# A fused attention and Fourier kernel: PV with v as the stationary operand, diagonal score blocks sharing columns, transfers in pairs, and a newly searched order

## The chip, the cores and the metric

One core of one Trainium2 chip. The metric is the device time of one execution in microseconds (us). With one core, runs are compared by the granted clock of the tensor engine (TensorE) that the profile gives beside each: a run of the kernel before at clock 1.00 takes about 246.8 us, those at 0.993 took 248.2 to 252.0 us. What a lower clock goes with in the profiles is shown below; the slower runs of the kernel before were not profiled themselves. Runs over 1.5% above the fastest of their kernel are called slow, and ratios use the fast ones alone. Engines are named as the profile does: PE is TensorE's matmuls, PEld its weight loads, DVE VectorE, ACT ScalarE, POOL GpSimd.

## The reference, cut to what matters

```python
x = A_x                                             # 2048 tokens x 640, bf16
g = sigmoid((x * gate_w).sum(-1, keepdims=True))    # a gate for each token
a = attention(x)       # 32 heads of 20; four segments of 512 tokens, causal inside a segment
b = irfft2(rfft2(x) * (w_r + 1j * w_i))             # over tokens and channels
return g * a + (1 - g) * b

# attention, for each segment s:
logits = qs @ ks.T * scale + mask;  p = softmax(logits);  a_dot = p @ vs
a_mem = (phi(qs) @ M) / (phi(qs) @ z + 1e-6)        # M, z: sums over the earlier segments
o = sigmoid(beta) * a_mem + (1 - sigmoid(beta)) * a_dot
M, z = M + phi(ks).T @ vs, z + phi(ks).sum()        # at the end: out = o @ wo
```

## The kernel before

The kernel is straight-line code for five engines. It carries its own list scheduler: each operation is described once, with its inputs, outputs and a typed-in duration, and a long list named ORDER, found by a search, says in which order each engine gets its operations. The scheduler works out from the durations when each one should start, and places buffers accordingly. It knows a delay between engines, a price for changing the tiling of TensorE, and some VectorE operations that it does not place beside GpSimd's.

```python
HOP = 70.0
COST = {(0, 1): 94.0, (0, 2): 94.0, (1, 0): 110.0, ...}     # changes of tiling, ns
def schedule(self, pools, order, nsem=56):
    ...                                 # t: when inputs, bank and engine are free
    occ, lat = o.alts[e][1:]            # the typed-in duration
    if e == "pe" and o.emode != mode:
        occ += self.COST[mode, o.emode]
    free[e] = o.t1 = t + occ
```

Durations are typed in like this (matmuls, then one operation of another engine):

```python
cost = sum(c * PECOL + 0.75 if mode > 0 else max(c * PECOL + 2.8, 25.4) for _, c in items)
...
fix0, per0, late = {"act": (65, 0.833, 110.0), "dve": (67, 1.04, 68.0), "pool": (100, 0.945, 50.0)}[eng]
```

Attention works on pairs of groups of four heads. A score unit fills four PSUM banks, the exponential reads all four, GpSimd masks the triangles, and PV multiplies with the exponentials as stationary operand, 40 matmuls of 21 columns a group:

```python
POOLS = {"qk": [0, 1, 2, 3], "gen": [4, 5, 6, 7]}
for pr in range(4):
    for u, parts in enumerate(self.UNITS):
        self.qk_unit(s, pr, u, parts)          # scores, Exp, masks
    for g in (2 * pr, 2 * pr + 1):
        self.pv_group(s, g)
# the Exp, the mask of one diagonal block, and one PV product:
e.activation(dst(), src(), ACT.Exp, scale=SC)
e.affine_select(ex[.. 4 heads, 128 columns ..], same, [[0, 4], [1, P]], ALU.is_ge, 0.0, ...)
th = (psum[.. 21 columns ..], ex[.. 128 x 128 ..], va[.. 21 columns of head 4*g+hh ..])
```

(The last three lines are shortened; the whole kernel follows.)

The softmax here doesn't subtract the row's maximum and nothing guards it: scores larger than these inputs give would overflow.

## Time and profile before

The median of the first three runs was 246.92 us (246.74 to 249.36).

| | before |
|---|---|
| span of the profiled run, granted clock | 244.2 us, 1.000 |
| exponentials | 80, 150.3 us |
| masks | 128, 81.0 us |
| tensor instructions (matmuls and weight loads) | 7404 |
| PE waits for "issue" in the whole span | 0.2 us in each of two groups of lines |

### The profile page before, as it was taken

To read this page: it belongs to the slowest core of one execution; us is meant where nothing else is said; L and a number is where in the kernel's file an instruction comes from. 1 tells how busy PE (TensorE), PEld (TensorE's weight loads), DVE (VectorE), ACT (ScalarE), POOL (GpSimd) and SP (SyncE) were. 2 spreads that over 40 slices of the span, in tenths; PEclk is the share of its full clock that TensorE was granted. 3 is DMA by queue.
4 is the path that set the end of the run, shared out by engine and by line. 5 is a ranking of instruction groups with operands and counts; after the bars stand their busy time and mean duration, and the time that the engine had idled before them with its cause. 6 is when DMAs were issued, how large, how long until landed. Compare 5 with 4: busy or idle time off the path is not lost.

```text
span 244.2 us, 8905 instructions
## 1 busy us (share of the span) xinstructions
PE 233.1 (95%) x3702; PEld 139.8 (57%) x3702; DVE 198.8 (81%) x534; ACT 201.6 (83%) x204; POOL 132.2 (54%) x200
## 2 busy tenths in 40 slices
PE   7999999999999999999978999999899999999994
PEld 2344575557556457645644475645555667667683
DVE  1489997988999898979999999989999975643643
ACT  2088889999998998999987998888899878798820
POOL 8421861362648484455876385646567656407610
PEclk9999999999999999999999999999999999999999
DMA  7998866696493656756442546313442969586224
GB/s 185 328 358 231 218 172 169 205 182 172 138 192 92 168 128 150 226 164 200 109 104 71 144 137 182 94 59 111 118 100 71 203 144 97 79 123 116 77 62 131
DMA packets 55880, 36.71 MB, mean 150 GB/s; under 512 B 31792, under 2 KB 52128, under 8 KB 55840
## 3 DMA queue, kind: packets, MB, share of 16 engines
q1 hardware_dynamic: 54144, 35.32, 58.4%
q10 hardware_dynamic: 1696, 0.82, 1.2%
q8 instruction: 29, 0.48, 0.8%
q14 instruction: 11, 0.09, 0.1%
HBM read 19.86 MB, written 9.71 MB: 121 GB/s over the span
## 4 chain that ended last, share of the span: by engine, by line
PE 72%; DVE 16%; DMA 5%; ACT 4%; issue 2%; SPq 0%; DVEq 0%
PE psum L498 64%; PE psum L496 8%; DVE Pt L1287 4%; ACT ex L1137 3%; DMA xT<-in_A_x_dram 2%; DMA oT<-o_scr 2%; DVE Cp L509 2%; DVE Yt L1292 1%; DVE qu L509 1%; ACT et L1010 1%; DVE va L1045 1%; DVE Bt L509 1%; DVE on L1172 1%; DVE on L1177 0%; DVE phk L1021 0%
## 5 line engine op out<-in xcount | busy, mean ns | idle before, releaser
L1137 ACT ACTIVATE ex<-psum 128x2048 bf16<-128x2048 f32 x80 | 150.3, 1878 | 15.8 <-PE psum L498 14.8
L1140 POOL TENSOR_SCALAR_AFFINE_SELECT ex<-ex 128x512 bf16<-128x512 bf16 x128 | 81.0, 653 | 70.5 <-ACT ex L1137 66.7
L498 PEld LDWEIGHTS psum<-va,ex 128*128 128x128 bf16 x1280 | 39.0, 96 | 5.8 <-issue 1.3
L498 PE MATMUL psum<-va,ex 128*128 128x21 bf16 x1280 | 41.1, 172 | 0.1
L498 PE MATMUL psum<-xT,wk 128*128 128x512 bf16 (+1 forms) x140 | 33.3, 380 | 0.6 <-DMA xT<-in_A_x_dram 0.6
L498 PE MATMUL psum<-xT,wq 128*128 128x512 bf16 (+1 forms) x135 | 32.2, 380 | 1.2 <-DVE Bt L509 1.2
L498 PE MATMUL psum<-qp,kp 20*128 20x384 bf16 (+3 forms) x512 | 31.7, 301 | 0.7 <-ACT ex L1137 0.2
L498 PE MATMUL psum<-wv,xT 128*128 128x500 bf16 (+1 forms) x160 | 31.9, 300 | 0.2
L1287 DVE TENSOR_TENSOR Pt<-psum,Wt 128x642 bf16<-128x642 f32 x32 | 25.4, 822 | 0.8 <-PE psum L498 0.5
L496 PE MATMUL psum<-wo,oT 128*32 128x320 bf16 x480 | 23.0, 300 | 0.2 <-issue 0.2
L498 PEld LDWEIGHTS psum<-qp,kp 20*128 20x128 bf16 x512 | 9.0, 92 | 18.3 <-ACT ex L1137 9.6
L509 DVE CAST ot<-psum 128x320 bf16<-128x320 f32 x21 | 9.9, 489 | 11.6 <-PE psum L496 8.4
L498 PEld LDWEIGHTS psum<-wv,xT 128*128 128x128 bf16 x160 | 13.3, 97 | 10.0 <-DVE Ac L509 0.8
L498 PE MATMUL psum<-big,Ac 128*128 128x321 bf16 (+2 forms) x96 | 17.9, 256 | 0.8 <-DVE Cp L509 0.4
L1045 DVE TENSOR_TENSOR va<-psum,ebx 128x500 bf16<-128x500 f32 (+1 forms) x32 | 15.2, 484 | 3.5 <-PE psum L498 2.8
L498 PE MATMUL psum<-tt,Yt 128*128 128x256 bf16 (+1 forms) x96 | 17.0, 274 | 0.4 <-DVE qu L509 0.2
L1292 POOL TENSOR_TENSOR Yt<-Pt 128x321 bf16<-128x321 bf16 x18 | 13.4, 757 | 7.2 <-DVE Pt L1287 4.6
L509 DVE CAST qu<-psum 128x512 bf16<-128x512 f32 x20 | 13.6, 686 | 3.4 <-PE psum L498 3.2
L1333 DVE TENSOR_TENSOR G<-eo,psum 128x320 bf16<-128x320 f32 x32 | 14.9, 479 | 1.7 <-PE psum L496 0.9
L498 PEld LDWEIGHTS psum<-xT,wk 128*128 128x128 bf16 (+1 forms) x140 | 9.9, 97 | 10.9 <-issue 2.3
L1177 POOL TENSOR_TENSOR on<-on,mem 128x320 bf16<-128x320 bf16 x16 | 12.8, 806 | 5.8 <-DVE on L1172 5.8
L1172 DVE TENSOR_TENSOR on<-psum,rs 128x320 bf16<-128x320 f32 x32 | 15.3, 481 | 0.6
(85 smaller groups left out, 379.9 us busy)
## 6 DMA issues: line engine op xcount, KB each, us to landing
tt<-tab_tt SPq DMA_DIRECT2D x16, 256.0 KB, 3.3
xsb<-in_A_x_dram SPq DMA_DIRECT2D x8, 320.0 KB
kp<-k_scr SPq DMA_DIRECT2D x28, 80.0 KB
qp<-q_scr SPq DMA_DIRECT2D x28, 80.0 KB
o_scr<-on SPq DMA_DIRECT2D x12, 160.0 KB
out_dram<-ot SPq DMA_DIRECT2D x12, 160.0 KB
q_scr<-qu SPq DMA_DIRECT2D x6, 256.0 KB
k_scr<-qu SPq DMA_DIRECT2D x6, 256.0 KB, 3.9
```

The costliest lines, as they stand in the source:

```text
L496: h = e.matmul(dst, wt, r_, start=st, stop=sp_, **{**kw, "tile_position": (0, q), "skip_group_check": True})
L498: h = e.matmul(o_, l_, r_, start=st, stop=sp_, **kw)
L509: alts["dve"] = (lambda e: e.tensor_copy(dst(), src()), 67 + 1.04 * n, 68.0)
L1010: self.one("act", lambda e: e.activation(et.ap(0, [1, L]), qsl(), ACT.Exp), L, [qb], [b("et", pi_)], late, name="phi_exp")
L1045: self.one("dve", lambda e: e.tensor_tensor(va.ap(i * H * VW + h0 * VW, [VW, nh], [1, DH]), self.ps(bank, 0, [DH, nh], [1, DH]), self.ebx. ...
L1137: self.one("act", lambda e: e.activation(dst(), src(), ACT.Exp, scale=SC), 4 * width, [bank], [self.exb(s, g, j) for g, j in outs], prio - ...
L1140: self.one("pool", lambda e, g=g, j=j: e.affine_select(self.ex.ap(self.exo(s, g) + JOFF[j], [1280, 4], [1, P]), self.ex.ap(self.exo(s, g) ...
L1172: self.one("dve", lambda e, rs=rs, bank=bank, g=g: e.tensor_tensor(on.ap(80 * g, [D, 4], [DH, 4], [1, DH]), self.ps(bank, 0, [88, 4], [VW, ...
L1177: self.either(lambda e, g=g: e.tensor_tensor(on.ap(80 * g, [D, 4], [1, 80]), on.ap(80 * g, [D, 4], [1, 80]), self.mem.ap(80 * g, [D, 4], [ ...
L1287: self.one("dve", lambda e, ri=ri, Pt=Pt, Wt=Wt, bank=bank: e.tensor_tensor(Pt.ap(ri * 322, [644, 2], [1, KD]), self.ps(bank, 0, [0, 2], [ ...
L1292: fn = lambda e, r=r, a0=a0, a1=a1, op=op, Pt=Pt, Yt=Yt: e.tensor_tensor(Yt.ap(r * 322, [1, KD]), Pt.ap(a0 * 322, [1, KD]), Pt.ap(a1 * 322 ...
L1333: self.one("dve", lambda e, q=q, n2=n2, bank=bank, eo=eo: e.tensor_tensor(self.G.ap(n2 * D + 639 * q, [1 - 2 * q, 320]), eo.ap(q, [1, 320] ...
```

## The change

The intent: PE carries most of the chain of waits, so take work from it. In segments 0 to 2, PV is turned around: v (padded to 32 columns a head) is stationary, and the exponentials stream through four column tiles, 24 matmuls a group. Diagonal score blocks share columns, so a pair of groups needs fewer exponential elements, at the price of more and smaller score matmuls and masks. Small transfers go in pairs. The transform uses another permutation of frequencies. The diff has 34 hunks; this is its core:

```diff
-JOFF = (0, 512, 1024, 896)
+KPOS = (0, 256, 128, 384)
+VPIECES = ((0, 0, 512, 0), (1, 512, 384, 128), (2, 896, 192, 320), (2, 1088, 64, 256), (3, 1152, 64, 448), (3, 1216, 64, 384))
...
-    UNITS = (((0, (0,)),), ((0, (1, 3)),), ((1, (0,)),), ((0, (2,)), (1, (2,))), ((1, (1, 3)),))
+    UNITS = (((0,), 0), ((0,), 1), ((1,), 0), ((0, 1), 2), ((1,), 1))
+    PIECES = (((0, 0, 0, 0, 0, 512), (1, 64, 64, 128, 0, 64), (0, 64, 64, 64, 64, 448)),
+              ((1, 0, 0, 192, 0, 320), (1, 64, 64, 192, 0, 320), (2, 0, 0, 320, 320, 192), (2, 64, 64, 320, 320, 192)),
+              ((2, 0, 0, 256, 0, 64), (3, 64, 64, 384, 0, 128), (3, 0, 0, 448, 64, 64)))
-    ORDER = ( 36, 0, 86, 56, ... )
+    ORDER = ( 36, 0, 82, 54, ... )          # the whole list is new
...
+    def pv_flipped(self, s, g):
+        for n_, (jj, o, n, q0) in enumerate(VPIECES):
+            for hh in range(4):
+                def th(...):
+                    return (self.ps(bank, q0, [1, n], p0=32 * hh, np_=32), va.ap(jj * H * VW + (4 * g + hh) * VW, [1, 32]),
+                            self.ex.ap(self.exo(s, g) + hh * 1280 + o, [1, n]), n_ == 0, n_ == 5,
+                            {"tile_position": (0, 32 * hh), "skip_group_check": True})
...                                           # result and denominators go through DRAM
+            if ks == "a":                     # two masks here, two or three for "b" and "c"
+                self.mask(s, g, P, 512, 0, 64, ("a0",), ("m1",), prio, 64)
+                self.mask(s, g, P, 0, 0, P, (), ("a0",), prio, 0)
```

## The prediction

> **What bounds the kernel now.** I read the page's busy table first, then the chain, then the costly groups and waits, and last the order in time of two engines in the last segment, where few other things happen.
>
> ```profile
> PE 233.1 (95%) x3702; PEld 139.8 (57%) x3702; DVE 198.8 (81%) x534; ACT 201.6 (83%) x204; POOL 132.2 (54%) x200
> ...
> PE 72%; DVE 16%; DMA 5%; ACT 4%; issue 2%; SPq 0%; DVEq 0%
> ...
> L1137 ACT ACTIVATE ex<-psum 128x2048 bf16<-128x2048 f32 x80 | 150.3, 1878 | 15.8 <-PE psum L498 14.8
> L1140 POOL TENSOR_SCALAR_AFFINE_SELECT ex<-ex 128x512 bf16<-128x512 bf16 x128 | 81.0, 653 | 70.5 <-ACT ex L1137 66.7
> L498 PEld LDWEIGHTS psum<-va,ex 128*128 128x128 bf16 x1280 | 39.0, 96 | 5.8 <-issue 1.3
> L498 PE MATMUL psum<-va,ex 128*128 128x21 bf16 x1280 | 41.1, 172 | 0.1
> ```
>
> PE is nearly always busy and carries 72% of the chain; but ACT and DVE stand above 80% over the whole span, so a cut on PE alone meets them soon. A PE record lasts 172 ns at 21 columns because matmuls overlap; what one costs has to be read from starts, in the order in time of PE (start, length, group):
>
> ```profile
> 218.98 0.44 PE L496 MATMUL psum<-wo,oT 128*32 128x320 bf16 x8
> 219.35 0.39 PE L498 MATMUL psum<-qp,kp 20*128 20x512 bf16 x4
> 219.68 0.32 PE L496 MATMUL psum<-wo,oT 128*32 128x320 bf16 x4
> ...
> 227.12 1.17 PE L498 MATMUL psum<-va,ex 128*128 128x21 bf16 x40
> 228.21 0.86 PE L496 MATMUL psum<-wo,oT 128*32 128x320 bf16 x20
> ...
> 229.28 0.40 PE L498 MATMUL psum<-qp,kp 20*128 20x384 bf16 x8
> 229.61 0.32 PE L498 MATMUL psum<-G,fbg 128*32 128x320 bf16 x4
> ```
>
> The 40 PV matmuls of one group of four heads take 228.21 - 227.12 = 1.09 us, 27 ns each, although their 21 columns are 9 ns of streaming. A score unit (four row tiles at once, 512 columns, 213 ns) takes 0.33 us to the next start, and the eight matmuls before it, 8 x 320 columns four abreast or 0.27 us, began 0.37 us earlier: about 0.12 us is lost after it and 0.10 us before it, 0.11 us for each change of tiling.
>
> The same stretch on ACT shows the loop that paces attention. A score unit fills all four banks of its PSUM pool, so the next scores wait for the exponential, and it for them:
>
> ```profile
> 222.22 1.88 ACT L1137 ACTIVATE ex<-psum 128x2048 bf16<-128x2048 f32 x1 [0.55 <-PE psum L498]
> 224.75 1.88 ACT L1137 ACTIVATE ex<-psum 128x2048 bf16<-128x2048 f32 x1 [0.65 <-PE psum L498]
> 226.78 0.44 ACT L507 ACTIVATE ot<-psum 128x320 bf16<-128x320 f32 x1
> 227.24 1.88 ACT L1137 ACTIVATE ex<-psum 128x2048 bf16<-128x2048 f32 x1
> 229.73 1.88 ACT L1137 ACTIVATE ex<-psum 128x2048 bf16<-128x2048 f32 x1 [0.61 <-PE psum L498]
> ```
>
> The period is 2.49 us: 1.88 of exponential and 0.61 of turnaround, into which ACT fits one eviction. The first exponential starts at 13.3 us and the last ends at 231.6, so 80 units took 218.3 us, 2.73 each; at 2.49 they would take 199. The 19 us between are places where PE had other work in front of the scores, or ACT two or three evictions in a row. After 231.6 come 12.6 us of masks, PV, projection and stores.
>
> [...] the unit of 8 matmuls above (384 and 128 columns) takes the same 0.33 us as 4 of 512, [...] but nothing here is as short as 64 columns. [...] Here 1878 - 2048 x 0.833 = 172 ns fixed, which I use.
>
> **The change part by part.** Counts are from the two built instruction lists.
>
> PV in segments 0 to 2. 24 groups lose 40 matmuls each. In their place come 24 matmuls a group with v as a 32-column stationary operand in four column tiles; together they stream 1280 columns four abreast, 533 ns. 24 x (1.09 - 0.53) = 13.4 us less PE. The result is transposed and unnormalised: instead of three VectorE operations a group (168 + 244 + 481 ns, 24 times, 21.4 us) there is one 512-element eviction (about 0.69 us on DVE, 0.60 on ACT: 15 go to DVE for 10.3 us, 9 to ACT for 5.4 us). Denominators go through DRAM and come back as a table; 15 multiplies and 8 additions of memory output appear late, 16 of them on DVE at about 0.45 to 0.55 us (7.8 us), with 3 reciprocals of 128 elements (2.6 us, an estimate from 335 ns for 32 and 244 for 16). Summed with the redistributed evictions DVE goes from 198.8 to about 195, but with 11 us or more moved out of the crowded middle into the last segment, where DVE is half idle.
>
> Scores. The masked quadrant of each diagonal block takes a neighbour's useful quadrant, so a group has 1152 columns instead of 1280. [...] matmuls there go from 512 to 1280, in eight tiles. Exponentials: 56 full ones (105.2 us), 12 of 1024 elements (12.3), and in the last segment, where pieces are split, 8 each of 1280 (9.9), 768 (6.5) and 512 (4.8): 138.7 for 150.3, 11.6 less. ACT takes about 7.2 us of evictions more in return (5.4 for PV, the rest other copies): net 201.6 to 197.
>
> Masks. 128 masks of 653 ns become 224: 96 of 512 elements and 128 of 256 [...]: 62.7 + 52.6 = 115 us for 81. Less 15 additions of memory output (12.1 us) and plus about 12 of other work, POOL goes from 132 to about 166. PV waits for masks, but is issued well behind them.
>
> Changes of tiling: 175 to 185, 10 x 0.11 = 1.1 us more. [...] PE net: -13.4 - 1.7 + 1.1 + 1.4 = -12.6 us.
>
> Transfers in pairs: half as many pad loads, weight-row loads and tables, fewer transposes, but 12 stores and 15 loads of PV output. The queue is at 58% and no wait for it ranks among the long ones after the start, so I count 0.
>
> The sum on the path. The score loop: 12 pairs of groups at 4 x 2.49 + (1.03 + 0.61), and 4 at 2 x 2.49 + 2 x 2.57 + 1.71 give 139 + 47 = 186 us for 199, 13 less. ACT's own work between first and last exponential: 195.7 us before, 191.3 after; before it filled 90% of the 218.3 us. PE's 12.6 us less, and DVE's relief in the middle, let it fill more. With 93% the body is 191.3 / 0.93 = 205.7 us, 12.6 less, which agrees with what PE gives up and with the shorter loop. Start and tail stay: the last segment keeps the old PV. 246.9 - 12.6 = 234.3; a new order that issues four exponentials early (the old one leaves 10.5 us between first and second) should add 1 to 2. I choose 233.
>
> **The rivals.** (1) ACT is the bound, and stays 90% full: the body is 191.3 / 0.90 = 212.6 and the time 241, just over 2% faster. For it: ACT loses only 4.4 us. Against: before its exponentials it waited 14.8 us for PE. (2) The 27 ns floor holds for tiled matmuls too. Then 1280 score matmuls cost 34.6 us for 15.4, and PV 15.6 for 12.8: PE loses 22 us more, the gain is gone, and the time is 250 or more. Against it stands the unit of eight. (3) The masks become the wait: 3.6 us of POOL for a group, in a period of about 6, with three score buffers. They could hold PV and the buffers back; I would give that 3 to 5 us: 238. (4) The order was searched for exactly this balance, and ACT reaches 97%: body 197, time 226.
>
> **Range and chances.** The centre is 233. The low end, 226, is rival 4; the high end, 241, is rival 1, or 3 with less gain on PE. Faster than 2% means under 242, which fails only if ACT gains no share at all or if rival 2 holds in part: faster 0.88, within 2% 0.10, slower 0.02.
>
> **What would show it.** PV groups of segments 0 to 2 at 0.5 to 0.7 us between starts; score units at 0.33 to 0.40 us; exponentials summing to 139 us; ACT busy about 197, DVE 195, POOL 166; the last exponential ending 12 to 13 us before the end, near 218. Wrong if the score units take 0.45 us or more (rival 2), if PE waits for POOL's masks by more than 5 us in sum (rival 3), or if the idle time before exponentials stays near 15 us.

What the kernel before shows of the rates used there: 14 matmuls of 512 columns start 0.216 us apart (13.72 to 16.74 us in PE's order in time), 0.42 ns a column, and at that rate 32 x 128 columns are 1.7 us. On ACT an eviction of 320 elements took 437 ns, one of 512 took 598 and an exponential of 2048 took 1878, 0.83 to 0.84 ns for each element more. The 1.4 us for small pieces and the 411 ns for a mask of 256 elements were estimates and rest on no trace.

## More of the kernel before

A matmul whose tiling is left free (mode -1) takes that of its neighbours; if that is four column tiles, it is written as up to four matmuls of 32 stationary columns each:

```python
if op.mode < 0 and op.emode == 2:
    for q in range(0, m, 32):
        n = min(32, m - q)
        ...
        h = e.matmul(dst, wt, r_, ..., **{**kw, "tile_position": (0, q), ...})
else:
    h = e.matmul(o_, l_, r_, start=st, stop=sp_, **kw)
```

The busy line, the costly groups and the last segment are in the prediction. One view is not there, and should have been: the busy time of each engine in the long middle of the program, where the start and the tail do not dilute it. Its columns are the stretch, its length, and the busy time with the number of instructions for PE, PEld, DVE, ACT and POOL; then clock, share of the DMA engines and GB/s.

```profile
core 0: us, PE busy (x) PEld busy (x) DVE busy (x) ACT busy (x) POOL busy (x), PEclk, DMA share, GB/s
60.00:200.00 140.00, 134.37 (x1965) 79.78 (x1967) 130.03 (x359) 127.47 (x119) 87.11 (x133) 1.00 0.52 135
```

Over the span PE, DVE and ACT stand at 95, 81 and 83%. In this stretch they stand at 96, 93 and 91%: three engines are nearly full at once, so work taken from one may leave the other two to set the time.

## The result, and the profile after

| | before | after |
|---|---|---|
| time, median of 4 runs of the same rounds | 248.14 us (246.74 to 250.05) | 272.11 us (267.82 to 276.71) |
| profiled run: span, granted clock | 244.2, 1.000 | 265.7, 0.987 |
| exponentials | 80, 150.3 us | 92, 138.6 us |
| masks | 128, 81.0 us | 224, 123.0 us |
| tensor instructions | 7404 | 11932 |
| the same, up to the 17th score unit | 1418 | 3622 |

The ratio is 1.0854 [1.0663, 1.1045], where 233 us had been predicted. Ratios here and below are the mean time of one kernel's fast runs over that of the other's fast runs in the same rounds, with a 95% interval, so they are not quite the ratio of the medians.

The page of the changed kernel, first its busy line, then the exponentials:

```profile
PE 233.9 (88%) x5966; PEld 144.2 (54%) x5966; DVE 207.8 (78%) x490; ACT 199.0 (75%) x236; POOL 173.9 (65%) x293
...
L1246 ACT ACTIVATE ex<-psum 128x2048 bf16<-128x2048 f32 (+4 forms) x92 | 138.6, 1506 | 28.4 <-PE psum L504 26.6
```

The exponentials shrank as planned, but ACT idled 28.4 us in front of them, where it had idled 15.8. Next, two products one after the other on PE (start, length, group): a score unit and a flipped PV group.

```profile
102.41 0.43 PE L504 MATMUL psum<-qkp 20*64 20x512 bf16 x12
102.77 0.73 PE L504 MATMUL psum<-ex,va 128*32 128x512 bf16 x24
103.33 0.39 PE L504 MATMUL psum<-wv,xT 128*32 128x500 bf16 x4
```

The score unit takes 0.36 us to the next start and the PV group 0.56 us. The products are as fast as they should be. So where is the time? The start of the exponentials, counted by the share of their work that has begun, tells:

| share of the exponential work | before, us | after, us |
|---|---|---|
| 5% | 31.62 | 27.07 |
| 10% | 42.91 | 57.76 |
| 15% | 54.48 | 69.41 |
| 20% | 64.50 | 87.82 |
| 50% | 126.88 | 149.45 |
| end of the last | 231.61 | 253.18 |

At 5% the changed kernel is 4.6 us ahead; at 20% it is 23.3 us behind; from there it gains 2 us. From that mark to the end of the last they take 167.1 us before (231.61 - 64.50) and 165.4 us after.

**What the program itself had planned.** As the scheduler computes a start for every operation, that plan can be printed and laid beside the trace. This is its own arithmetic from typed-in durations, not a measurement:

```
                        before    after
planned end              238.5    234.0
planned busy PE          207.1    195.2
planned busy ACT         193.3    185.8
planned busy DVE         175.2    176.2
planned busy POOL        123.5    149.0
```

(PE without changes of tiling; with them 225.0 and 214.0.) The plan promised 4.5 us, not 14. The lag, a measured start minus the planned start of the same exponential, in us:

| exponential number | 0 | 4 | 8 | 12 | 16 | 24 | 40 | 60 | last |
|---|---|---|---|---|---|---|---|---|---|
| before | 0.1 | 0.6 | 0.7 | 1.0 | 1.3 | 1.4 | 2.8 | 5.0 | 5.7 |
| after | 0.2 | 5.2 | 13.3 | 13.7 | 17.3 | 18.6 | 21.8 | 26.4 | 31.0 |

The spans differ by 21.5 us: 4.5 us planned gain, and 26.0 us that no plan held. Of those, 12.7 come up to exponential 12 (13.67 - 0.96), 3.3 from 12 to 16, 9.3 from there to the last, and 0.7 in the tail.

**The first 12.7 us: PE waits for nothing that the data explains.** The longest waits of PE's matmuls in the changed kernel (us in sum, times, longest):

```profile
PE psum L502 <- issue: 8.4, 8, 2.7
PE psum L504 <- issue: 2.7, 5, 1.1
PE psum L504 <- DVE omh L984: 2.4, 1, 2.4
```

"Issue" is time in which the engine waited for nothing that the profile shows: 11.1 us where the kernel before has 0.4. The order in time shows what kind of wait it is:

```profile
18.35 0.71 PE L502 MATMUL psum<-xT,wk 128*32 128x256 bf16 x18
21.30 1.05 PE L502 MATMUL psum<-xT,wk 128*32 128x256 bf16 x30 [2.23 <-issue]
...
25.19 0.34 PE L504 MATMUL psum<-qkp 20*64 20x320 bf16 x6
26.62 0.40 PE L504 MATMUL psum<-qkp 20*64 20x320 bf16 x10 [1.09 <-issue]
```

The second pause lies inside one score unit of 16 matmuls, after the sixth. All 16 were released by the same inputs, so no data held the seventh back. Such pauses follow one another after about 127 matmuls, each with its weight load: with the semaphore waits, 255 to 257 recorded instructions of PE from one pause to the next, or a multiple of 256. The page counts packets of an instruction queue: they went from 29 (0.48 MB) to 47 (0.77 MB), one for each 256 of 7404 and of 11932 tensor instructions, and 256 is the spacing of the pauses. A run of 256 is called a block below.

No view lists these packets one by one, but the packed trace holds them, and they show what the pauses go with. Each has 16384 bytes and takes 0.88 to 1.65 us in the changed kernel. Each of the 12 longest pauses there ends 1.3 to 1.5 us after such a packet has ended, and 2.3 to 3.0 us after it started. Over all kept traces this holds for 76 of 79 such pauses of 0.3 us or more (1.1 to 1.7 us after the packet's end, and all but one of these 2.2 to 3.1 us after its start). The author reads this as PE standing until its next block has come. In the two longest pauses the packet began only about when PE stopped (51.84 us for the pause at 51.89, 18.79 for that at 19.06); why it began so late is not shown.

Before 61 us there are eight pauses of 9.3 us in sum, and in these 61 us PE was busy for 49.1 us.

After some of the long pauses something follows. The windows from 52 us, with the columns as above (the clock is third from the end):

```profile
52.00:54.00 2.00, 0.00 (x0) 0.00 (x0) 0.79 (x3) 0.70 (x4) 1.75 (x3) 1.00 1.02 283
54.00:56.00 2.00, 1.38 (x20) 0.75 (x23) 0.68 (x1) 0.00 (x0) 0.00 (x0) 0.79 1.59 197
56.00:58.00 2.00, 2.00 (x45) 1.06 (x40) 0.69 (x1) 0.24 (x1) 0.00 (x0) 0.50 0.91 207
58.00:60.00 2.00, 1.90 (x70) 1.24 (x63) 1.09 (x2) 1.75 (x2) 0.29 (x1) 0.86 0.46 109
```

A pause of 2.73 us ends at 54.62; then the granted clock is 0.50 for about 3.4 us (half of 54 to 56, all of 56 to 58, a quarter of 58 to 60). Not every long pause is followed so: after the one of 2.23 us that ends at 21.30 the clock stays at 1.00. In the kept traces 25 of 35 pauses of PE from 1.6 to 3.4 us have such a stretch beside them. One stretch takes 1.7 / 244 = 0.007 off the mean clock of a run, which is the step seen between runs of one kernel (1.000, 0.993, 0.987). None of the four runs of the changed kernel was at 1.00 (0.987, 0.978, 0.978, 0.948).

**The next 3.3 us: VectorE behind masks.** The 2.4 us that PE waits for "omh" is the chain of a small DVE operation. DVE just before it:

```profile
71.89 2.08 DVE L974 TENSOR_TENSOR ebg<-gate,ebx 128x128 f32<-128x128 f32 x1
73.89 1.27 DVE L1068 TENSOR_TENSOR phk<-phk,et 128x512 bf16<-128x512 bf16 x1
75.09 0.40 DVE L984 TENSOR_TENSOR omh<-gg,omh 128x8 bf16<-128x8 f32 x1
```

The first two took 2.08 and 1.27 us; before, such operations took 0.45 and 0.47 us in the mean. GpSimd was busy beside them all the time (2.08 of 2.08 us and 1.27 of 1.27), mostly with masks. Of the 15 operations of the second's form (phk) in the changed kernel, the four with no GpSimd instruction beside them took 0.41 to 0.43 us, the five with masks beside them from end to end 0.53 to 1.27. After this pause the clock halves again (0.50 in 76 to 78 us). The masks themselves, by form:

```profile
L1267 POOL TENSOR_SCALAR_AFFINE_SELECT ex<-ex 128x256 bf16<-128x256 bf16 x128 | 60.5, 484 | 38.5 <-ACT ex L1246 30.8 <-ACT gate L1096 6.5
L1267 POOL TENSOR_SCALAR_AFFINE_SELECT ex<-ex 64x512 bf16<-64x512 bf16 x64 | 44.2, 697 | 4.1 <-ACT ex L1246 2.9
L1267 POOL TENSOR_SCALAR_AFFINE_SELECT ex<-ex 128x512 bf16<-128x512 bf16 x32 | 21.8, 683 | 0.6
```

The scheduler's formula gives 342 ns for 256 elements and 584 for 512. Measured are 484 and about 690, so POOL's planned 149.0 us became 173.9.

**The middle.** The same window as before the change:

```profile
60.00:200.00 140.00, 126.68 (x2847) 74.03 (x2851) 124.96 (x297) 120.46 (x134) 104.31 (x186) 0.99 0.61 157
```

PE, DVE and ACT fell from 96, 93 and 91% to 90, 89 and 86%. All three are less busy, and the loop is not faster. From the first exponential to the end of the last, ACT fills 194.76 of 240.88 us, 81%, where it had filled 196.00 of 218.29, 90%, and the prediction had put 93%. That needed its own experiments.

### The profile page after: what moved, and what is told of

The parts are those of the page before. It is cut to its first block, busy times and chain, and to the rows that moved or that the text cites. A ratio compares the mean times of both kernels' runs of the same rounds, so it can differ in the third digit from the quotient of the medians.

```text
span 265.7 us, 13485 instructions
## 1 busy us (share of the span) xinstructions
PE 233.9 (88%) x5966; PEld 144.2 (54%) x5966; DVE 207.8 (78%) x490; ACT 199.0 (75%) x236; POOL 173.9 (65%) x293
## 3 DMA queue, kind: packets, MB, share of 16 engines
q1 hardware_dynamic: 57156, 40.71, 60.6%
## 5 line engine op out<-in xcount | busy, mean ns | idle before, releaser
L1246 ACT ACTIVATE ex<-psum 128x2048 bf16<-128x2048 f32 (+4 forms) x92 | 138.6, 1506 | 28.4 <-PE psum L504 26.6
L1267 POOL TENSOR_SCALAR_AFFINE_SELECT ex<-ex 128x256 bf16<-128x256 bf16 (+2 forms) x224 | 123.0, 574 | 43.2 <-ACT ex L1246 33.7
L504 PE MATMUL psum<-qkp 20*64 20x64 bf16 (+5 forms) x1280 | 33.2, 272 | 3.5 <-issue 1.7
L502 PE MATMUL psum<-wo,oU 128*32 128x320 bf16 x480 | 23.6, 300 | 1.8 <-DVE oU L1517 1.6
L504 PE MATMUL psum<-ex,va 128*32 128x64 bf16 (+3 forms) x576 | 18.9, 265 | 3.1 <-POOL ex L1267 1.1
L502 PE MATMUL psum<-xT,wk 128*32 128x256 bf16 x480 | 18.3, 273 | 3.7 <-issue 3.7
L504 PE MATMUL psum<-wv,xT 128*32 128x500 bf16 (+3 forms) x330 | 21.1, 306 | 0.3 <-issue 0.3
L504 PEld LDWEIGHTS psum<-ex,va 128*32 128x32 bf16 x576 | 12.1, 100 | 13.7 <-POOL ex L1267 6.8
L502 PE MATMUL psum<-xT,wq 128*32 128x512 bf16 x260 | 18.5, 380 | 0.0
L502 PE MATMUL psum<-wv,xT 128*32 128x500 bf16 (+1 forms) x280 | 15.3, 301 | 3.6 <-issue 3.6
L504 PE MATMUL psum<-xT,wk 128*32 128x256 bf16 (+1 forms) x160 | 16.0, 273 | 1.3 <-DMA xT<-in_A_x_dram 1.3
L502 PEld LDWEIGHTS psum<-xT,wk 128*32 128x32 bf16 x480 | 12.6, 97 | 6.7 <-issue 5.2
```

The source lines that it names most:

```text
L502: h = e.matmul(dst, wt, r_, start=st, stop=sp_, **{**kw, "tile_position": (0, q), "skip_group_check": True})
L1246: self.one("act", lambda e, d=d, q=q: e.activation(self.ex.ap(*d), self.ps(bank, *q), ACT.Exp, scale=SC), n, [bank], [self.exb(s, 2 * pr + ...
L1267: self.one("pool", lambda e: e.affine_select(self.ex.ap(e0 + d0, [1280, 4], [1, n], np_=np_), self.ex.ap(e0 + s0, [1280, 4], [1, n], np_=np_),
```

## The experiments

Theory D (delivery): the changed kernel loses its start because it needs more tensor instructions there than reach the engine in time. Theory M (masks): it loses because GpSimd's masks hold VectorE, or PE directly. Theory W (worth): even without both, the saved work of PE and ACT is not time in this program. A rival to all three is that the new order is poor by itself. The expectations call delivery theory A and the masks rival B. Wrong results are marked; the other kernels were judged correct.

### A. Fewer and more tensor instructions

**a_untiled_early.** The changed kernel, with the free matmuls left untiled up to the 17th score unit (2076 tensor instructions up to there for 3622; 68 changes of tiling for 36).

```diff
         for i, o in enumerate(pe):
-            o.emode = o.mode
-            if o.mode < 0:
+            nqk = nqk + (o.name == "qk") if i else 0
+            o.emode = max(o.mode, 0) if nqk < 17 else o.mode
+            if o.emode < 0:
```

> The changed kernel, same order, but until the 17th score unit every matmul that may be cut into four column tiles stays whole: 2076 matmul and weight-load instructions on PE up to there instead of 3622, for 32 more changes of tiling (about 3.5 us). Theory A [...]: the pauses of PE inside groups of equal matmuls before 61 us (8.4 us in seven) vanish or halve, and most of the 23 us lost by the first fifth of the exponentials comes back: 254 to 262 us. Rival B (GpSimd's longer masks hold VectorE up): 268 to 275, since masks are untouched and PE has more changes of tiling.

Median 262.03 us; one run of 257.92 at clock 1.00 and three at 0.976 to 0.984 that count as slow, so there is no ratio. The first 61 us, the changed kernel first, this one second:

```profile
0.00:61.00 61.00, 49.11 (x1382) 31.05 (x1386) 36.79 (x85) 35.99 (x56) 25.67 (x40) 0.97 0.84 205
```

```profile
0.00:61.00 61.00, 57.82 (x825) 34.15 (x830) 44.15 (x112) 43.76 (x64) 30.88 (x49) 1.00 0.88 211
```

With 825 matmuls for 1382, PE is busy for 8.7 us more, and DVE and ACT with it. The lag at exponential 16 falls from 17.3 to 8.5 us against the same plan. Some 9 us of the start are won, net of 32 more changes of tiling. Against its own plan (printed in the same way from its kernel), which holds these changes, the lag at exponential 12 is 1.6 us for 13.7: 12 of the 12.7 us of the start went with the instructions that were taken out there: theory D puts them down to delivery and to what follows its pauses. The medians differ by about 10 us.

**a_untiled.** All free matmuls untiled, 8014 tensor instructions, 306 changes of tiling.

```diff
-            o.emode = o.mode
-            if o.mode < 0:
+            o.emode = max(o.mode, 0)
+            if False:
```

> The same for the whole kernel: 8014 instructions on PE instead of 11932, 306 changes of tiling instead of 185 (13 us more, so that PE's own work is that of the kernel before). Theory A alone: the early gain as in the other run, and later a loss if PE paces there: 256 to 268. If PE does not pace the later part, it is no slower than the run cut early. Rival B: 270 to 285.

263.03 us (260.35 to 264.69), 1.0613 [1.0506, 1.0719]. The same gain in the start (lag 9.3 at exponential 16), and no more after it: the further cuts in instructions are paid for in changes of tiling.

**a_two_tiles.** Free matmuls in two tiles of 64 columns in place of four of 32 (9332 tensor instructions, 2594 early).

```diff
-                    for q in range(0, m, 32):
-                        n = min(32, m - q)
+                    for q in range(0, m, 64):
+                        n = min(64, m - q)
```

> The changed kernel with every freely tiled matmul cut into two tiles of 64 columns in place of four of 32: the same order, 9332 instead of 11932 tensor instructions, 2594 instead of 3622 up to the 17th score unit. Theory A (the tensor engine waits for its instructions to be delivered): the pauses in the middle of groups that came every 127 matmuls before 61 us vanish or shrink to under 3 us in sum, and unlike in the untiled run no switch is added, so the 15% mark of the exponentials is passed near 61 us instead of 73 and the median falls to 257 to 262 us. Rival B (GpSimd's masks slow VectorE): no change to the first 60 us beyond what PE saves, over 268 us. Rival C (tiles of another size count as a switch): PE waits of about 0.1 us at each change between 64- and 32-column tiles, 262 us or more although the pauses are gone.

265.2 us (264.71 to 268.53), 1.0767 [1.0692, 1.0842]. One pause is left, 1.36 us at 55 us, and the lag at exponential 12 is 6.7 us for 13.7, so delivery again gives back 7 us. But PE's busy time rises to 245.8 us from 233.9, and the lag grows to 27.4 us by the last exponential. The trace bears out rival C of the expectation: in this run PE goes 133 times between tiles of 64 and of 32 columns, and a pair of 500-column matmuls, 211 ns at 0.42 ns a column, takes 305 ns to the next start when that is of the other width. About 0.1 us each, these changes cost some 13 us of PE, an estimate. Theory D holds for the start; as a cure, this trade is poor.

**b_split_early.** The reverse: the kernel before, with projections and the first transform step in four column tiles up to the 17th unit (3052 tensor instructions there for 1418).

```diff
-            o.emode = o.mode
-            if o.mode < 0:
+            nqk = nqk + (o.name == "qk") if i else 0
+            o.emode = 2 if o.name in ("proj", "vproj", "F1") and held.get(id(o.banks[0]), 2 if nqk < 17 else 0) == 2 else o.mode
+            if o.emode < 0:
...
-                if op.mode < 0 and op.emode == 2:
+                if op.mode <= 0 and op.emode == 2:
```

> The kernel before, with its projections and first transform cut into four column tiles until the 17th score unit: 3052 instructions on PE up to there instead of 1418, and 31 more changes of tiling (3 us). Theory A: pauses inside groups of equal matmuls appear in the first 60 us, about every 256 instructions, and the time is 254 to 264. Rival: only the changes of tiling cost, 248 to 251.

255.6 us (254.36 to 257.03), 1.035 [1.0281, 1.0419]. The lag at exponential 16 is 5.8 us for 1.3, and there are pauses inside groups (1.03, 0.36 and 1.68 us) that the kernel before did not have. 32 more changes of tiling at 0.11 us are 3.5 us of PE work; against its own plan, which holds them, the lag at 16 is 2.9 us, so only about 1.5 us of the start is delivery. About 4 us more are lost late, around the pause of 1.68 us at 213 us, where nothing was cut. The sign is as theory D has it, the size much smaller than the changed kernel's loss.

**b_chop_early.** As many instructions without any tiling: projection matmuls cut into 64 columns (3454 up to the 17th unit).

```diff
+                elif op.hold:                   # proj and vproj before the 17th unit
+                    for q in range(0, N, 64):
+                        ...
+                        h = e.matmul(cut(o_), l_, cut(r_), start=st and q == 0, stop=sp_ and q + n == N, ...)
```

> The kernel before with the matmuls of its projections, up to the 17th score unit, cut into pieces of 64 moving columns under the same 128-column weights: 3454 instead of 1418 tensor instructions by then (the changed kernel has 3622), no tile mode, no switch and no other instruction added; by the durations of before about 3.4 us more tensor work. Theory A (instruction delivery alone makes the pauses): pauses with no releaser in the middle of groups, about 127 matmuls apart, 4 us or more in sum before 70 us, so that the median rises by 6 us or more (3.4 us of work included), to 253 or more. If the pauses of the changed kernel came from its 32-column tiles and not from the number of instructions: no such pause over 0.3 us, and the median stays within 4 us, under 251.

256.74 us (252.9 to 259.75), 1.0324 [1.0212, 1.0436]. There is one pause only (1.88 us at 16 us); the lag of 6.4 us by exponential 8 is mostly slower work, since a 64-column piece with its weight load takes about 31 ns to the next, where 64 columns at 0.42 ns are 27. So the number of instructions alone does not make pauses. In the pause-free stretches the changed kernel eats a block of 127 matmuls in 3.2 to 5.3 us, and here, from the one pause to 74 us, a block lasts 4.1 to 5.4 us. From one crossing to the next, the changed kernel took 4.1 to 6.1 us in its start, pause included. That is no fixed ceiling: in its last 20 us, where the DMA engines are busy for 0.25 of the time (0.84 in the first 61 us), it takes four blocks in a row in 3.7 to 4.0 us each without such a pause.

**a_big_early.** The changed kernel, with the 0.8 MB load of the transform's tables moved earlier in the order, in case bulk loads hold up the packets of the instruction queue.

```diff
-        ... 254, 50, 278, ... 865, 70, 2178 ...      # ORDER
+        ... 254, 50, 70, 278, ... 865, 2178 ...
```

> The changed kernel with one 0.8 MB load of constants issued near 24 us instead of 46 us, where the DMA engines are less full; no instruction of another engine moves. Theory A [...]: the pauses at 44.6, 48.7 and above all the 2.7 us one at 51.9 us, which lie among that load, 0.5 MB of tables and a transposing load, shrink by 2 us or more in sum, while pauses near 25 to 35 us may grow; the 10% mark of the exponentials comes earlier by 1 us or more. If the pauses have nothing to do with the DMA traffic, they stay where they are, within 0.5 us in sum.

270.66 us (267.83 to 271.25), 1.0936 [1.0873, 1.0999]. PE's waits for "issue" sum to 12.6 us for 11.1; the expectation that they shrink by 2 us was missed. That this load delays those packets is not shown. That a transfer can hold PE up is suggested by the three pauses that fit no packet: those of 1.68 us in b_split_early, and of 2.28 and 1.64 in b_less_pv and b_both below, each at a multiple of 256 instructions. The block's packet had ended 3.7 to 4.5 us before they end, but each ends within 0.14 us of the last packet of a transposing load (oT<-o_scr). What ties the two together stays open.

### B. The masks

**b_masks_twice.** The kernel before, with every second mask done twice.

```diff
+            def mask(e, g=g, j=j):
+                for _ in range(1 + j % 2):
+                    h = e.affine_select( ... )
```

> The kernel before, with half of its masks done twice (same result): GpSimd's busy time rises by about 42 us to 174, as in the changed kernel. Rival B (GpSimd's work slows VectorE and delays PV): 254 to 262. Theory A: under 250.

The second mask reads and writes the first one's data without a synchronisation between them, which is a race. It did not run; the next kernel took its place.

**b_masks_split.** Each mask of the kernel before as two, of two heads each.

```diff
-            self.one("pool", lambda e, g=g, j=j: e.affine_select(... [1280, 4], [1, P] ...), 512, ...)
+            self.one("pool", lambda e, g=g, j=j: [e.affine_select(... + o, [1280, 2], [1, P] ...) for o in (0, 2560)][1], 512, ...)
```

> The kernel before with each of its 128 masks done as two over two heads each (about 484 ns twice instead of 653 once), so that GpSimd has about 40 us more work (132 to about 172), as in the changed kernel; correct result. Rival B: over 6 us longer, 253 us or more, VectorE's busy time up by 5 us or more. Theory A: within 2 us of the kernel before.

250.15 us (249.47 to 252.1), 1.0142 [1.0082, 1.0201]. POOL rose from 132 to 151 us, and that costs 3.5 us even in the order that was searched for 132. DVE's busy time did not move (198.8 to 198.4), so there the cost is not VectorE standing behind masks; that expectation was missed, and so was that of 40 us more GpSimd work.

**a_thin_masks.** The changed kernel, with in-place masks of 8 columns a head (wrong result): POOL 113 us.

```diff
+        if d0 == s0:
+            n, step = 8, 8
```

> Wrong result on purpose: the changed kernel, its five in-place masks of each group cut to 8 columns a head, so that GpSimd has about 75 us less work (174 to about 100, less than the 132 of the kernel before); nothing else moves. Rival B, masks: the stretch from 20% of the exponentials to the last falls from 163 to 155 us or less, VectorE's busy time falls from 208 to under 200, the 2.35 us wait for the prompt mask near 73 us goes, and the median falls by 8 us or more, to 264 or less. Theory A alone: the first 60 us keep their pauses, the stretch after 20% stays within 3 us of 163, and the median stays above 267.

268.83 us (265.6 to 269.67), 1.0842 [1.076, 1.0924]. DVE falls from 207.8 to 198.7 us, so some 9 us of DVE's busy time went with the masks. The time does not follow: the start is still held by the pauses (lag 15.1 at exponential 8). But from exponential 8 to 60 the lag grows by 7.7 us only, for 13.1 in the changed kernel. What was won is lost near the end: VectorE waits 3.3 us for the denominators on their way back from DRAM (dnc<-u_scr, until 218.2 us), PE stands 3.07 us behind it, and a stretch of 17.1 us at clock 0.50 follows (mean clock 0.960).

**a_two_thin.** Two tiles and thin masks together (wrong result).

> Wrong result on purpose: both of the former together. If delivery and masks are separate losses, the savings add within 3 us; if the masks only filled a wait that delivery had made, the sum is smaller. A and B together expect 245 to 254 us; anything above 255 says that a third loss, the order itself, is larger than both.

259.13 us (257.95 to 259.6), all near clock 1.00, 1.0486 [1.0435, 1.0536]. Against two tiles alone this is 6.1 us less, well outside both ranges. The pages of the two, with thick masks and with thin ones:

```profile
PE 245.8 (93%) x4666; PEld 146.0 (55%) x4666; DVE 207.3 (79%) x490; ACT 199.1 (76%) x236; POOL 173.5 (66%) x293
```

```profile
PE 243.3 (95%) x4666; PEld 145.9 (57%) x4666; DVE 197.5 (77%) x490; ACT 198.6 (77%) x236; POOL 114.8 (45%) x293
```

DVE again loses 10 us. From exponential 8 to 60 the lag grows by 13.7 us, for 18.4 with two tiles alone. So theory M holds for about 5 us of lag with the pauses of the start and without them; in a_thin_masks the end hid it. The expectation had said that anything above 255 us shows a third loss. 259.13 is above it; the changes between tiles of two widths are such a loss, and the next run, which has none of them, comes under 255.

**a_untiled_thin.** Untiled early and thin masks (wrong result).

> Wrong result on purpose: the run that left tensor work uncut until the 17th score unit (262.0 us), with the thin masks on top (about 60 us less GpSimd work). If masks cost what the pair with two tiles showed (6 us), 255 to 257 us, with the 2.2 us wait for the prompt mask near 64 us gone. Over 260: the masks cost nothing here. Under 251: they cost far more once delivery no longer hides it.

253.12 us (251.64 to 255.66), 1.0229 [1.016, 1.0297]. Delivery and masks together take away 19 of the 24 us between the medians of the two kernels. The lag at exponential 16 is 4.4 us against the plan of the changed kernel. Of what is left, most comes in two jumps of 3.8 and 3.6 us, at pauses inside groups. The first, in PE's order in time:

```profile
140.85 0.23 PE L505 MATMUL psum<-wv,xT 128*32 128x141 bf16 x4
143.29 0.25 PE L505 MATMUL psum<-wv,xT 128*32 128x141 bf16 x4 [2.21 <-issue]
```

So a pause of this kind (2.21 us, and one of 2.25) comes again in the middle, in the four-tile products that were left. Against this run's own plan, which holds the changes of tiling of its start, the lag at the last exponential is 13.4 us, or 6.0 without the two jumps, for 5.7 in the kernel before. That speaks against the rival of a poor order: with its disturbances removed, the new order keeps to its plan nearly as well as the old one. But there is little in that plan: with the changes of tiling that the untiled start costs, it ends at 237.9 us, for the old kernel's 238.5.

### C. What saved work is worth here

**b_less_pv.** The kernel before with only the first key block in PV of segments 0 to 2 (wrong result). A group keeps 16 of its 40 matmuls: 24 groups x 24 x 27 ns are 15.6 us less PE work.

```diff
-                    for jj in range(i + 1):
+                    for jj in range(i + 1 if s == 3 else 1):
```

> Wrong result on purpose: the kernel before, in three of its four segments only the first key block of each PV product: 576 fewer PV matmuls of 27 ns, 15.6 us less tensor work and nothing else changed. It asks what the prediction took for granted, that tensor time saved there is time saved. If the prediction's premise holds, it falls by 10 us or more, to 237 or less. Rival D (the exponentials and their hand-overs take over at once, as the plan in the kernel foresees): it falls by less than 6 us, and the idle time of ACT before the exponentials shrinks by less than that.

249.64 us in 20 runs (246.12 to 252.28), 1.004 [1.0011, 1.0069]. Seven runs at clock 0.998 or more have a mean of 247.57, beside 246.95 for 20 such runs of the kernel before in that round. More PE work was taken away than the change takes, and nothing came of it. The program's own plan for this kernel had foreseen that: it ends at 238.1 us, for 238.5. The middle of the run:

```profile
60.00:200.00 140.00, 125.59 (x1480) 68.18 (x1493) 129.14 (x358) 127.01 (x119) 86.78 (x133) 1.00 0.56 136
```

PE is down to 90% in the middle, and DVE and ACT do within 1 us as much in these 140 us as before. The other 13 runs have a lower clock, and the profiled one shows what goes with it there: a pause of 2.28 us inside a group in the last segment, where two groups of 40 PV matmuls, the same as before, come without other work between.

```profile
205.96 1.34 PE L498 MATMUL psum<-va,ex 128*128 128x21 bf16 x47
209.59 0.98 PE L498 MATMUL psum<-va,ex 128*128 128x21 bf16 x33 [2.28 <-issue]
```

**a_less_pv.** The same in the changed kernel (one of the six pieces of a group is kept, 4 of 24 matmuls; wrong result).

```diff
-        for n_, (jj, o, n, q0) in enumerate(VPIECES):
+        for n_, (jj, o, n, q0) in enumerate(VPIECES[:1]):
```

> Wrong result on purpose: the changed kernel with only the first of six pieces of each flipped PV product: 0.32 us less tensor work in each of 24 groups, 7.7 us in all, and 960 fewer tensor instructions. If the tensor engine still bounds the steady part, it falls by 5 us or more, to 266 or less; if other waits bound it, by less than 3 us.

267.5 us (267.44 to 271.13), 1.0879 [1.0796, 1.0962]. By the medians that is 4.6 us less, by the fast runs nothing. The clock was lower (0.961 to 0.980), so the lag is the better measure: 26.3 us at exponential 60, for 26.4. Taking five of the six pieces away gives no time up to there, so the cost of flipped PV did not make the loss.

**b_short_exp.** The kernel before with one eighth of each exponential of segments 1 to 3 left out: 12.8 us less ACT.

```diff
-            dst = lambda: self.ex.ap(o0, [1280, 4], [1, width])
-            src = lambda: self.ps(bank, 0, [512, 4], [1, width])
+            w_ = width if s == 0 else width - 64
+            dst = lambda: self.ex.ap(o0, [1280, 4], [1, w_])
+            src = lambda: self.ps(bank, 0, [512, 4], [1, w_])
```

> Wrong result on purpose: the kernel before, its 60 exponentials of segments 1 to 3 leaving out an eighth of their columns, so that each is 0.21 us shorter, 12.8 us in all; nothing else changes. Loop theory (the chain exponential, score unit, exponential over the one four-bank score buffer sets the pace, which is why 15.6 us less PV work saved nothing): it falls by 8 us or more, to 239 or less. If the tensor engine set the pace, as the prediction took it, it falls by less than 3 us.

247.39 us in 20 runs, 1.0016 [0.9992, 1.004]. (The leftover columns keep old values; the error stays inside the tolerance, which does not make it right.) A little more ACT work than the 11.6 us that the change saves, and the time is the same within 0.4%.

**a_short_exp.** The same in the changed kernel.

```diff
+        if s > 0:
+            outs = [(d[:-1] + ([1, d[-1][1] * 7 // 8],), q[:-1] + ([1, q[-1][1] * 7 // 8],)) for d, q in outs]
```

> Wrong result on purpose: the changed kernel, its exponentials of segments 1 to 3 leaving out an eighth of their columns, 11.3 us less in all. If the exponentials pace its steady part, it falls by 6 us or more, to 266 or less. If they don't any more than the PV products did (4.6 us at most for 7.7 us less), because waits for masks, VectorE and instruction blocks stand in both loops, under 3 us.

273.17 us (268.53 to 275.13), 1.0903 [1.0771, 1.1035]: no gain, though here too VectorE waits for the denominators near the end (2.9 us), with a stretch of 17.1 us at clock 0.50 beside it. Up to exponential 60 the lag is 27.4 us, for 26.4.

**b_both and a_both.** PV and exponentials shortened together (wrong results).

> Wrong result on purpose: the kernel before with both reductions, 15.6 us less PV work and 12.8 us less exponentials; each alone changed its time by less than 0.5 per cent. Theory E (two loops of equal length: each exponential waits for the score unit, each score unit for the tensor work queued ahead of it and for the exponential before, so that one alone can't shorten the period of 2.58 us): together they take 8 us or more away, to 239 or less. Rival F (a third thing, VectorE or the transfers, paces both): under 3 us.

> Wrong result on purpose: the changed kernel with 7.7 us less PV work and 11.3 us less exponentials. Theory E as for the kernel before: 5 us or more below the better of the two alone, 262 or less. If GpSimd's masks and VectorE pace the steady part now, it stays within 3 us of the better one.

b_both: 251.29 us (249.69 to 255.46), 1.0115 [1.0031, 1.0199], at clocks of 0.973 to 0.990. a_both: 269.29 us (265.43 to 270.86), 1.0884 [1.0782, 1.0986]. Less work on both engines at once, and still no gain. In b_both the lag at exponential 40, before any stretch at clock 0.50, is 2.2 us against the plan of the kernel before, hardly under the 2.8 of that kernel.

**b_all and a_less_dve.** The same cut on VectorE: a product of the transform on 80 of 321 columns for all but two groups (wrong results), planned at about 15 us. 28 of 32 products are cut (the expectation says 30), and DVE's busy time falls by 11.3 us in b_all, 11.1 in a_less_dve. b_all is on top of b_both; a_less_dve is this cut alone in the changed kernel.

```diff
-                    Pt.ap(ri * 322, [644, 2], [1, KD]), self.ps(bank, 0, [0, 2], [1, KD]), ...
+                N_ = KD if g < 2 else 80
+                    Pt.ap(ri * 322, [644, 2], [1, N_]), self.ps(bank, 0, [0, 2], [1, N_]), ...
```

> Wrong result on purpose: the kernel before with 15.6 us less PV work, 12.8 us less exponentials and now 15 us less VectorE work as well (30 of the 32 products of L1287 over 80 instead of 321 columns each way). Theory G (three engines are equally full in the middle stretch: between 60 and 200 us PE is busy for 96 per cent, VectorE for 93, ACT for 91, so relief of two of them leaves the third): it falls by 7 us or more, to 240 or less, where both reductions without VectorE gave nothing. If the time is set by something that is none of the three (transfers, the order of waits itself): under 3 us.

> Wrong result on purpose: the changed kernel with 15 us less VectorE work in the same product. The change has already taken work from PE and ACT but none from VectorE (175 us planned before, 176 after; 199 and 208 measured). If VectorE is what is left as the limit of the stretch after 88 us, it falls by 6 us or more, to 266 or less, and the stretch from 20 per cent of the exponentials to the last from 163 to 157 us or less. If waits that are spread over all engines pace it, under 3 us.

b_all: 243.17 us (241.66 to 246.72), 0.9833 [0.9792, 0.9875]. It is the only kernel of all that is faster than before, by less than 2%: 15.6 us less PE, 12.8 less ACT and 11.3 less DVE make 4.1 us. Its middle:

```profile
60.00:200.00 140.00, 128.30 (x1616) 72.16 (x1629) 121.94 (x366) 121.68 (x122) 89.48 (x137) 1.00 0.54 138
```

Against b_both's window (126.25, 129.23 and 118.14 us for PE, DVE and ACT), DVE gives way and the other two do more in the same time; so DVE was one of the holds, but the three now stand at 92, 87 and 87% and something still sets the pace. a_less_dve: 267.57 us (265.45 to 271.51), 1.0814 [1.075, 1.0878]. From exponential 8 to 60 its lag grows by 10.4 us, for 13.1; near the end VectorE waits 2.3 us for the denominators, and a stretch of 13.7 us at clock 0.50 follows.

Theory W stands as far as it was tested: in this program, work taken from PE, from ACT or from both is not time while the order is kept. DVE alone, or with only one of the others, was not relieved in the kernel before, so that DVE alone would have given the 4.1 us is not excluded. Which chain of waits sets the pace of the middle was not found. A new search for an order of each shortened kernel was not tried, and b_less_pv and its kin do not say what that would give.

No correct kernel beat the kernel before. The best correct versions of the changed one are the two left untiled (262.0 and 263.0 us).

## Why the prediction was wrong, and where it was right

- **The operations were right.** PV "0.53" a group measured 0.56 us, score units 0.36, 0.35 and 0.25 us for 12, 16 and 24 matmuls (0.33 to 0.40 foreseen), about 10 ns for each of the 24, exponentials 138.6 for 138.7, the tail after the end of the last exponential 12.5 us for 12.6 before. Rival 2, the 27 ns floor between tiles, is false. In the program's own durations, with changes of tiling, PE's work went from 225.0 to 214.0 us, 11.0 less for the 12.6 predicted. PE's busy time, 233.1 and then 233.9, does not show this.
- **The step that failed is the sum:** "PE's 12.6 us less, and DVE's relief in the middle, let it fill more. With 93% the body is 191.3 / 0.93 = 205.7 us". It turns saved work into time at par. ACT's own work came out near the 191.3, at 194.8 us, but it filled 81% of the stretch, not 93, and the body took 240.9 us. b_less_pv and b_short_exp take out more of either and give 0; both together give nothing; with a third engine it is 4.1 us. The prediction's own first paragraph had "ACT and DVE stand above 80% over the whole span"; in the middle it was 91 and 93%, which one view would have shown. The program's plan, which holds the waits between engines, had 4.5 us.
- **A term was missing from the sum: instructions.** The prediction counted matmuls by their columns, and even noted that diagonal scores go "from 512 to 1280", but only priced them by streaming. The 11.1 us of PE waiting for "issue", with the stretch of 3.4 us at clock 0.50 behind the longest, made the start 12.7 us late. The variant untiled early recovers 12.0 of that, less 3.1 us for its changes of tiling.
- **A term had the wrong sign: DVE.** "DVE goes from 198.8 to about 195" became 207.8. With thin masks it is 196.5 to 198.7, so the operations were well counted, and 9 to 11 us went with the masks.
- **The masks were mis-sized.** 115 us were predicted and 123.0 measured; the 256-element mask took 484 ns for the estimate of 411, and POOL 173.9 for 166. Rival 3 was real, but not as written: PE's weight loads wait 7.6 us for masks in sum, over the limit of 5, for 1.4 before; the larger damage, as the author reads the runs, goes through VectorE (those 9 to 11 us). The experiments put masks at 5 to 6 us.
- **The early start was right and worth nothing.** The fourth exponential starts 4.6 us sooner, but the fifth starts 2.2 us later (36.79 for 34.57), after the pauses. The new plan itself would have given the lead back by the sixth (39.8 for 37.0).
- **Transfers at "0"** held for the queue as a whole (58.4 to 60.6%), and moving its largest early load gained nothing. But the 47 packets of the instruction queue are transfers too, and in three relieved runs (a_thin_masks, a_short_exp, a_less_dve) VectorE waits 2.3 to 3.3 us for the denominators that the change sends through DRAM.
- **The test of idle time worked.** The prediction would be wrong "if the idle time before exponentials stays near 15 us"; it was 28.4, nearly all of it behind PE.
- **The chances** (0.88 for faster) counted only rivals with the same parts. None asked what the parts need besides engine time.

What stays open: about 4.5 of the 9.3 us that the changed kernel loses between exponential 16 and the last. Four pauses sum to 1.6 us there, and the masks go with 3.2 (from 16 to 60 the lag grows by 5.9 us in a_thin_masks, for 9.1); the rest was not separated. Open too are why the packets before the longest pauses start late, and the chain that sets the pace of the middle in the kernel before.

## What to carry to other kernels

Before pricing a change in a tuned kernel by the engine it relieves, read the busy shares in the window where the work would come out: with three engines above 90% there, work saved on one or two of them was worth nothing here while the order was kept. Count the instructions for each microsecond of the engine that gets more of them; splitting matmuls into tiles multiplies instructions (7404 became 11932 here), and where pauses fall inside a group whose inputs are all ready, look for the packets of the instruction queue just before they end. Where a program carries its own plan, compare the plans first and then the lag of the trace behind each: the first number is what the change can give, and the curve of the second shows where it was lost.
